# Gated attention and feed-forward on one core: V as 16 high and 15 low parts in one 32-column weight tile, with steps of 64 keys of eight heads

## The chip, the cores and the metric

The kernel runs on one core of one Trainium2 chip. The metric is the time of one execution on the device in microseconds (us). Three runs of the kernel before gave a median of 1062.46 us (1061.37 to 1062.55).

## The reference

```python
def reference(A_x, A_wq, A_wk, A_wv, A_wo, B_x, B_w1, B_w2, gate_w):
    q = (x @ wq).reshape(B, S, H, Dh).transpose(0, 2, 1, 3)
    k = x @ wk
    v = x @ wv
    scores = einsum("bhqd,bkd->bhqk", q, k) * (Dh ** -0.5)
    p = softmax(scores, axis=-1)
    o = einsum("bhqk,bkd->bhqd", p, v)
    a = o.transpose(0, 2, 1, 3).reshape(B, S, H * Dh) @ wo
    h = silu(einsum("bsd,df->bsf", x, w1))
    b = einsum("bsf,fd->bsd", h, w2)
    g = sigmoid((x * gate_w).sum(-1, keepdims=True))
    return g * a + (1 - g) * b
```

x is 2048 x 512 (S = 2048 positions, D = 512), there are H = 32 heads of Dh = 16, one key and one value head for all of them, and F = 1792 features in the feed-forward part. Everything is f32. The result has to be as precise as f32 products, so the kernel writes most operands as a sum of a high and a low 16-bit part and multiplies three times (high x high, high x low, low x high).

## The kernel before

**Engines.** TensorE (PE) multiplies, ScalarE (ACT) takes exponentials, VectorE (DVE) splits, normalises and adds, SyncE (SP) issues most DMAs, GpSimd (POOL) clears tiles and issues the loads of weights. Each works through its own list in order. The order on every engine is written out by the kernel.

**Start.** `first_pass` loads x, transposes it, makes K and V for all positions, the first blocks of Q and bounds for the exponent's shift. `V(c)` (L419 to L425) transposes V into `VF`, an f32 tile of 16 key blocks by 32 columns: 16 columns of V and a column of ones, which gives the softmax's sum. `v_parts` (L342) makes `VH` and `VL`, its high and low f16 parts. Q goes to DRAM (`qd`) and comes back through `load_q` (L260), which fills a tile `qb` with high and low parts for both halves of the partitions; `sh` holds the shifts.

**Attention.** 512 queries (c) of eight heads (o) make a Q block. `rounds` (c, o, rb) has 32 entries: each is four of these eight heads, and its steps go over 16 key blocks of 128 keys, so that there are 512 steps. A round's heads are spread over the two row halves of the array (f) and two tiles in turn (p). In a step `scores` (L1018) multiplies K by Q twice (j = 0, 1; eight matmuls of 32 keys each, one of eight places of the array each, which run side by side), into the PSUM tile S (two buffers), and ACT takes exp of it into P (f32, 128 keys by four heads by 512 queries, four buffers). `pv` (L1058) multiplies P with V, one matmul for each of four heads and each half of the 128 keys, so the two halves of the keys stand in two PSUM tiles, `pv0` and `pv1`.

**Split and native steps.** The loop takes two steps in a turn (256 turns in all). The second step of a turn is always native: one f32 pass with `VF`. The first is split where DVE has room (`split_step`): the upper 16 bits of P, read as bf16 in place (`upper`, a stride of two), are multiplied by `VH` and by `VL`, and the low part L = P - upper(P), made by DVE in f16 (`low`, L1053), by `VH`. A step over the first key block of a round is native.

**Slots.** A turn's order on PE is a string: S is a score block, F an eight-matmul slot of the other work (feed-forward, Q blocks, output projection), P a pass of the split step before, B a bound, N a native pass. `SPLIT = "SFFFSFFFSPPPSBN"` is the plain one; `DENSE` and `WIDE` ones have more F. After each turn `fill` (L794) issues waiting DVE work against a budget in us: the evictions' second halves, weight splitting (`split_pieces`), checks of ranges (`chores`), and the rest of the normalising.

**A round's end.** `norm_a` (L970) transposes `pv0` and `pv1` into T and U, adds them, takes the reciprocal of the sum column and multiplies, into half of C. After the second of two rounds `norm_b` transposes C and `norm_c` splits it into O for the output projection. At a round's start `prefetch` issues the load of the next round's Q tile.

**Second pass.** If a range check fails, the whole is done again with scales taken from the data. It doesn't run with these inputs.

## Time and profile before

| | |
|---|---|
| median of three runs | 1062.46 us |
| span of the profiled execution | 1063.5 us |
| PE busy | 1047.1 us (98%) |
| ACT busy | 1013.2 us (95%) |
| DVE busy | 821.4 us (77%) |
| POOL busy | 26.8 us (3%) |
| exp (L1031) | 1024 instructions, 972.0 us busy |
| low parts (L1053) | 194 instructions, 443.2 us busy |
| PV passes with f16 or bf16 (L1075) | 3 x 1552 matmuls |
| granted TensorE clock, mean | 0.995 |

A line of the timeline has a start in us from the span's start, a length in us, the engine, the line of the kernel, the operation, what it writes and reads, the shapes, and how many like instructions were merged; in brackets stands an idle time of the engine ahead of it and what ended it. A group's line has the busy time in us and the mean length of one in ns, then the idle time ahead of its instructions. Matmuls of one slot run side by side in eight places of the array, so the length of one says little; the distance from one slot's start to the next is what a slot costs.

### The profile page before, as it was taken

To read this page: it belongs to the slowest core of one execution; us is meant where nothing else is said; L and a number is where in the kernel's file an instruction comes from. 1 tells how busy PE (TensorE), PEld (TensorE's weight loads), DVE (VectorE), ACT (ScalarE), POOL (GpSimd) and SP (SyncE) were. 2 spreads that over 40 slices of the span, in tenths; PEclk is the share of its full clock that TensorE was granted. 3 is DMA by queue.
4 is the path that set the end of the run, shared out by engine and by line. 5 is a ranking of instruction groups with operands and counts; after the bars stand their busy time and mean duration, and the time that the engine had idled before them with its cause. 6 is when DMAs were issued, how large, how long until landed. Compare 5 with 4: busy or idle time off the path is not lost.

```text
span 1063.5 us, 66447 instructions
## 1 busy us (share of the span) xinstructions
PE 1047.1 (98%) x31517; PEld 662.6 (62%) x31517; DVE 821.4 (77%) x925; ACT 1013.2 (95%) x1118; POOL 26.8 (3%) x56
## 2 busy tenths in 40 slices
PE   8999999999999999999999999999999999999996
PEld 6575777755555577665765567676665575555753
DVE  6787888878887788888888697887887774757775
ACT  6899999999999999999999999999999999999993
POOL 1110010000000000000000000000000000000000
PEclk9999999999999999999999999999999999999998
DMA  6322111100001000000000000000000100000001
GB/s 222 115 61 61 51 47 53 50 21 22 4 21 41 21 23 10 16 11 22 13 11 31 29 26 12 12 22 12 18 8 12 41 22 11 12 11 5 12 4 44
DMA packets 20706, 32.99 MB, mean 31 GB/s; under 512 B 5001, under 2 KB 11914, under 8 KB 20426
## 3 DMA queue, kind: packets, MB, share of 16 engines
q1 hardware_dynamic: 17338, 20.20, 5.8%
q0 software_dynamic: 2512, 8.13, 2.6%
q8 instruction: 248, 4.06, 1.6%
q10 hardware_dynamic: 576, 0.33, 0.1%
q14 instruction: 32, 0.26, 0.1%
HBM read 20.12 MB, written 8.52 MB: 27 GB/s over the span
## 4 chain that ended last, share of the span: by engine, by line
PE 92%; ACT 3%; DVE 2%; DMA 1%; issue 0%; SPq 0%; DVEq 0%; ACTq 0%
PE pv L1075 36%; PE pm L778 33%; PE S L1028 20%; ACT P L1031 3%; DMA xn<-in_A_x_dram 1%; PE pm L782 1%; PE pk L395 1%; PE pt L321 0%; DVE T L974 0%; DVE mxs L139 0%; DVE U L975 0%; DVE acc L759 0%; DVE T L976 0%; DVE C L981 0%; PE pm L352 0%
## 5 line engine op out<-in xcount | busy, mean ns | idle before, releaser
L1031 ACT ACTIVATE P<-S 128x1024 f32<-128x1024 f32 x1024 | 972.0, 1051 | 19.8 <-PE S L1028 7.7
L1028 PE MATMUL S<-qb,KT 50*32 50x512 f16 x8192 | 477.7, 378 | 1.1 <-ACT P L1031 1.0
L1053 DVE TENSOR_TENSOR L<-P 128x2048 f16<-128x2048 f32 x194 | 443.2, 2285 | 44.5 <-ACT P L1031 44.2
L1075 PE MATMUL pv<-P,VF 64*32 64x512 f32 x5088 | 353.4, 589 | 0.0
L1028 PEld LDWEIGHTS <-KT 50*32 50x32 f16 x8192 | 191.6, 90 | 188.7 <-issue 120.8
L778 PE MATMUL pm<-w2s,H 64*32 64x512 f16 x5376 | 268.4, 375 | 0.7 <-DVE e L827 0.4
L778 PE MATMUL pm<-xs,w1s 64*32 64x512 f16 x5376 | 244.2, 375 | 0.8 <-DVE acc L759 0.8
L778 PEld LDWEIGHTS <-H 64*32 64x32 f16 x5376 | 143.6, 93 | 47.5 <-issue 13.0
L778 PEld LDWEIGHTS <-w1s 64*32 64x32 f16 x5376 | 136.1, 93 | 43.5 <-issue 11.8
L1075 PEld LDWEIGHTS pv<-P,VF 64*32 64x32 f32 x5088 | 115.2, 107 | 29.7 <-issue 6.7
L827 DVE SCALAR_TENSOR_TENSOR e<-e,pm 128x512 f32<-128x512 f32 x56 | 38.5, 687 | 82.1 <-ACT e L826 81.8
L1075 PE MATMUL pv<-P,VH 64*32 64x512 bf16 x1552 | 91.7, 388 | 0.0
L1075 PE MATMUL pv<-P,VL 64*32 64x512 bf16 x1552 | 91.3, 385 | 0.0
L1075 PE MATMUL pv<-L,VH 64*32 64x512 f16 x1552 | 89.6, 374 | 0.2
L778 PE MATMUL pm<-xs,wqs 64*32 64x512 f16 x1152 | 81.4, 375 | 0.6 <-DVE qx L862 0.6
L1075 PEld LDWEIGHTS <-VH 64*32 64x32 f16 x3104 | 64.9, 93 | 22.5 <-issue 1.5
L778 PE MATMUL pm<-wo_s,O 64*32 64x512 f16 x1440 | 63.4, 375 | 0.0
L974 DVE STREAM_TRANSPOSE T<-pv 128x512 f32<-128x512 f32 x32 | 23.0, 717 | 41.4 <-PE pv L1075 30.1
L759 DVE SCALAR_TENSOR_TENSOR acc<-pm,g,acc 128x512 f32<-128x512 f32 x47 | 35.0, 744 | 19.6 <-PE pm L778 19.4
L778 PEld LDWEIGHTS <-wqs 64*32 64x32 f16 x1152 | 39.7, 92 | 13.1 <-issue 4.4
L125 DVE TENSOR_TENSOR H<-e,H 128x512 f16<-128x512 f32 x56 | 38.8, 692 | 1.9
L1075 PEld LDWEIGHTS <-VL 64*32 64x32 f16 x1552 | 32.6, 94 | 11.2
(162 smaller groups left out, 466.7 us busy)
## 6 DMA issues: line engine op xcount, KB each, us to landing
qb<-qd SPq DMA_DIRECT2D x192, 32.0 KB
raw<-in_B_w_dram POOLq DMA_DIRECT2D x23, 256.0 KB, 3.0
xn<-in_A_x_dram SPq DMA_DIRECT2D x8, 512.0 KB
out_dram<-acc SPq DMA_DIRECT2D x15, 256.0 KB
qd<-qx SPq DMA_DIRECT2D x12, 256.0 KB
raw<-in_A_wo_dram POOLq DMA_DIRECT2D x4, 256.0 KB, 3.2
qb<-sh SPq DMA_DIRECT2D x62, 2.0 KB
raw<-in_B_w_dram SPq DMA_DIRECT2D x3, 256.0 KB
```

Of the source, the lines that this page charges most:

```text
L125: nc.vector.tensor_tensor(a2, a, a1, op=OP.subtract)
L395: nc.tensor.matmul(pk[64 * h:64 * h + 64], wkvs[:, i, kt], xs[:, j, kt, (c + h) * 512:(c + h) * 512 + 512], start=kt + n == 0, stop=kt == ...
L759: nc.vector.scalar_tensor_tensor(a, po, gate[:, n:n + 1], a, op0=OP.mult, op1=OP.add)
L778: nc.tensor.matmul(self.bank[32 * m:32 * m + 32], l(i, rows, 32 * m), r(j, rows), start=first, stop=last)
L782: nc.tensor.matmul(self.bank, l(i, slice(0, 128), 0, 128), r(j, slice(0, 128)), start=first, stop=last)
L827: nc.vector.scalar_tensor_tensor(e, e, 1.0, ph, op0=OP.add, op1=OP.mult)
L974: nc.vector.transpose(T, pv[0])
L1028: nc.tensor.matmul(sc[32 * m:32 * m + 32, f], KT[b:b + 50, k0:k0 + 32], qtile[i][b:b + 50, j], start=True, stop=True)
L1031: nc.scalar.activation(P[:, 2 * j:2 * j + 2], sc, AF.Exp, scale=scale_of(c, o))
L1053: nc.vector.tensor_tensor(lows[s], P, upper(P), op=OP.subtract)
L1075: nc.tensor.matmul(pvs[i][h][32 * j:32 * j + 32], a[r], b[r, j], start=first, stop=last)
```

## The change

V's low part gets into the 32 columns that a weight tile has anyway: column 0 is ones, columns 1 to 16 the high parts of V's 16 columns, and 17 to 31 low parts of the first 15. The sixteenth low part is written into the others: `v_parts` rounds the high parts to a common grid for each key and moves small multiples of the grid's step from low columns to high ones, so that a sum of column 16 and the first twelve low columns with weights 1, -1/2, -1/4 ... (`nus`; formed by `norm_x` and `norm_y`) gives the sixteenth column back. So a split step needs two passes, upper(P) and the low part, both with the one tile `VP`.

With high and low columns of the same keys side by side, a step now takes 64 keys of all eight heads, not 128 keys of four: 16 rounds of 32 steps, 512 as before, and each half of the partitions holds the same keys for other heads. `VF` and `VP` have 32 key blocks, each stored in both halves; `V(c)` makes them by matmuls with the identity as the moving operand, 64 columns each. A Q tile holds eight heads (twelve DMAs, sixteen with shifts), and its prefetch is issued in the middle of a round. The low part of P goes into the lower 16 bits of P itself, as f16. V is packed inside the attention part (`pack`, with `fill`); a split step waits for it in the order (`packed`), so the first turns are native. Normalising is done once for eight heads, in three parts over several turns.

```diff
-SPLIT, NATIVE = "SFFFSFFFSPPPSBN", "SFFFSFFFSNBSN"
+SPLIT, NATIVE = "SFFFSFFFSPPSBN", "SFFFSFFFSNBSN"
...
-    VH = consts.tile([128, NKT, 32], F16)
-    VL = consts.tile([128, NKT, 32], F16)
-    VF = consts.tile([128, NKT, 32], F32)
+    NK = S // 64
+    VP = consts.tile([128, NK, 32], F16)
+    nus = consts.tile([128, 3, 16], F32)
+    VF = consts.tile([128, NK, 32], F32)
...
-    qb_ = [consts.tile([128, 2, 512], F16, name=f"qb{n}") for n in range(2)]
+    qb_ = [consts.tile([128, 2, 2, 512], F16, name=f"qb{n}") for n in range(2)]
...
+            for r in range(2):
+                nc.sync.dma_start(q[b:b + 16, r], v[f][:, r, :, 0])
+                nc.sync.dma_start(q[b + 16:b + 32, r], v[f][:, r, :, 0])
+                nc.sync.dma_start(q[b + 32:b + 48, r], v[f][:, r, :, 1])
+                if shifts:
+                    nc.sync.dma_start(q[b + 48:b + 48 + shifts, r], u[f][0:shifts, r])
...
+    def v_parts(tiles, half):
...
+        def first():
+            absmax(u, V)
+            nc.vector.tensor_scalar(u, u, 1.0 + 2.0 ** -9, 1e-30, op0=OP.mult, op1=OP.max)
+            nc.vector.tensor_scalar(u.bitcast(U32), u.bitcast(U32), 0x7F800000, None, op0=OP.bitwise_and)
+            ts(u, u, 2.0 ** -10)
+            ts(h, u, 0.5)
+            ts(m, u, MAGIC)
+            tt(hi, V, to(h), OP.subtract)
+            tt(hi, hi, to(m), OP.add)
+
+        def second():
+            tt(hi, hi, to(m), OP.subtract)
+            tt(lo, V, hi, OP.subtract)
+            tt(s, lo, nu, OP.mult)
+            nc.vector.tensor_reduce(w, s, axis=AX.X, op=OP.add)
...
+        def fifth():
+            tt(VP[:, these, 1:17], hi, k, OP.add)
+            tt(VP[:, these, 17:32], lo[:, :, 0:15], k[:, :, 0:15], OP.subtract)
...
-                pt = ps.tile([128, KD, 128], F32, name="pt", bufs=4)
-                for t in range(4):
-                    o = c * 256 + t * 128
-                    nc.tensor.transpose(pt[:, t], vr[:, o:o + 128], ident)
+                for a in range(2):
+                    pt = ps.tile([128, KD, 128], F32, name="pt", bufs=4)
+                    for t in range(4):
+                        o = c * 256 + a * 256 + t * 64
+                        for e in range(2):
+                            nc.tensor.matmul(pt[64 * e:64 * e + 64, t], vr[:, o:o + 64], ident, start=True, stop=True)
...
+            if extra:
+                extra.pop(0)()
+                room -= 1.8
...
-                    k0 = kt * 128 + 32 * m
-                    nc.tensor.matmul(sc[32 * m:32 * m + 32, f], KT[b:b + 50, k0:k0 + 32], qtile[i][b:b + 50, j], start=True, stop=True)
+                    k0 = kt * 64 + 32 * (m % 2)
+                    nc.tensor.matmul(sc[32 * m:32 * m + 32, f], KT[b:b + 50, k0:k0 + 32], qtile[i][b:b + 50, m // 2, j], start=True, stop=True)
...
-                lows[s] = wp.tile([128, 4, 512], F16, name="L", bufs=2)
+                lows[s] = half(probs[s], F16, 0)
...
-                nc.vector.tensor_tensor(lows[s], P, upper(P), op=OP.subtract)
+                nc.vector.tensor_tensor(lows[s], P, half(P, BF, 1), op=OP.subtract)
...
-                a = (VH, VL, VH)[n][:, k]
-                b = lows.pop(s) if n == 2 else upper(probs[s])
+                a = VP[:, k]
+                b = lows.pop(s) if n else half(probs[s], BF, 1)
...
+        def norm_a(pv, st):
+
+            st["T"] = wp.tile([128, 32, 32], F32, name="T2")
+            for n in range(2):
+                nc.vector.transpose(st["T"][:, 16 * n:16 * n + 16].rearrange("p a b -> p (a b)"), pv[n])
+
+        def norm_x(st):
+            T3 = st["T"]
+            nc.vector.tensor_tensor(T3[:, :, 1:16], T3[:, :, 1:16], T3[:, :, 17:32], op=OP.add)
+            d = T3[:, :, 16:17 + DIG]
+            w = st["w"] = wp.tile([128, 512], F32, name="U")[:, 0:32 * (1 + DIG)].rearrange("p (a b) -> p a b", a=32)
+            nc.vector.tensor_tensor(w, d, nus[:, 1:2, 0:1 + DIG].to_broadcast([128, 32, 1 + DIG]), op=OP.mult)
+
+        def norm_y(st):
+            T3 = st["T"]
+            nc.vector.tensor_reduce(T3[:, :, 16:17], st["w"], axis=AX.X, op=OP.add)
+            r = wp.tile([128, 32, 1], F32, name="rr")
+            nc.vector.reciprocal(r, T3[:, :, 0:1])
...
+                norm_a(pvs.pop(i), state)
+                spend(1.4)
+                put(1.3, 1, lambda: norm_x(state))
+                put(1.6, 1, lambda: norm_y(state))
+                put(0.65, 3, lambda: (norm_b(state), put(1.0, 3, lambda: norm_c(state, (c, o)))))
...
+            if on and steps[s][1] == NKT:
+                prefetch(steps[s][0] + 1)
```

More of the change, by code (lines that the diff above doesn't have):

```diff
@@ L481, in first_pass @@
             next(q0)
[L482 removed]
+            load_q(qb_[0], 0, 0, 0)
             place(0)
@@ L604, in second_pass @@
             nc.vector.tensor_scalar(zsc, xk, -1.0, None, op0=OP.mult)
[L606 to L608 removed]
+            pv_ = ps.tile([128, NK, 32], F32, name="pv_", bufs=1)
+            for t in range(NK):
+                for e in range(2):
+                    nc.tensor.matmul(pv_[64 * e:64 * e + 64, t], kr[32:64, t * 64:t * 64 + 64], ident[32:64, 32:64], start=True, stop=True)
             vm = sb.tile([128, 1], F32)
@@ L1037, in split_step @@
         def split_step(s):
-            return steps[s][1] > 0 and backlog[0] < 0.8 and (dense_[0] or not (turn[0] and turn[0].hidden and (0 < turn[1] <= 6 or wide[0])))
+            return steps[s][1] < packed[0] and steps[s][1] > 0 and backlog[0] < 0.8 and (dense_[0] or not (turn[0] and turn[0].hidden and (0 < turn[1] <= 6 or wide[0])))
         def low(p, s, j):
@@ L1062, in pv @@
                 pvs[i] = [pO.tile([128, 512], F32, name=f"pv{h}") for h in range(2)]
-            first, last = k == 0 and n in (0, 3), k == NKT - 1
+            first, last = k == 0 and n in (0, 3), k == NK - 1
             if n == 3:
@@ L1093, in early_products, with pack @@
                 yield
+        def pack():
+            t2 = wp.tile([128, 32, 32], F32, name="T2").rearrange("p a b -> p (a b)")
+            tiles = [wp.tile([128, 512], F32, name="U"), t2[:, 0:512], t2[:, 512:1024]]
+            for half in range(2):
+                extra.extend(v_parts(tiles, half))
+                extra.append(lambda: packed.__setitem__(0, packed[0] + NKT))
+        packed, extra = [0], []
         qtile, wide = {}, [False]
```

143 lines of the change are left out of this document (78 added, 65 removed).

## The prediction, made before the changed kernel had run

> **What bounds the kernel now.** I read the page first, then ACT's timeline, then PE's timeline in one steady stretch, then DVE's groups and the two ends of the run.
>
> ```profile
> span 1063.5 us, 66447 instructions
> ...
> PE 1047.1 (98%) x31517; PEld 662.6 (62%) x31517; DVE 821.4 (77%) x925; ACT 1013.2 (95%) x1118; POOL 26.8 (3%) x56
> ...
> PE 92%; ACT 3%; DVE 2%; DMA 1%; issue 0%; SPq 0%; DVEq 0%; ACTq 0%
> ...
> L1031 ACT ACTIVATE P<-S 128x1024 f32<-128x1024 f32 x1024 | 972.0, 1051 | 19.8 <-PE S L1028 7.7
> ```
>
> The chain of work that ended last runs over PE for 92% of the span, so PE sets the pace. But ACT is busy for 95%. The question is how much room PE's shortening finds before ACT is the limit, and the next view answers it.
>
> ```profile
> 32.73 1.94 ACT L1031 ACTIVATE P<-S 128x1024 f32<-128x1024 f32 x2 [0.72 <-PE S L1028]
> ...
> 300.24 7.46 ACT L1031 ACTIVATE P<-S 128x1024 f32<-128x1024 f32 x8
> 307.51 0.67 ACT L826 ACTIVATE e<-pm 128x512 f32<-128x512 f32 x1
> 307.99 25.27 ACT L1031 ACTIVATE P<-S 128x1024 f32<-128x1024 f32 x27
> ...
> 964.11 79.75 ACT L1031 ACTIVATE P<-S 128x1024 f32<-128x1024 f32 x86
> ```
>
> The attention part lasts from the first exp at 32.73 to 964.11 + 79.75 = 1043.86 us. It has 1024 exps, four in each turn of the step loop (a turn is two steps of the loop over key blocks). When PE lets it, ACT does eight exps in 307.51 - 300.24 = 7.27 us, so 0.909 each and 3.64 a turn; a tanh adds 307.99 - 307.51 = 0.48 (4.12 a turn). The last row shows 79.75 / 86 = 0.927, so 3.71 a turn: there something other than ACT's own speed sets the pace. PE's rows of the same stretch show what.
>
> ```profile
> 1008.14 0.60 PE L1075 MATMUL pv<-P,VH 64*32 64x512 bf16 x8
> 1008.37 0.60 PE L1075 MATMUL pv<-P,VL 64*32 64x512 bf16 x8
> 1008.60 0.59 PE L1075 MATMUL pv<-L,VH 64*32 64x512 f16 x8
> 1008.84 0.57 PE L1028 MATMUL S<-qb,KT 50*32 50x512 f16 x8
> 1009.05 1.21 PE L1075 MATMUL pv<-P,VF 64*32 64x512 f32 x16
> 1009.91 0.57 PE L1028 MATMUL S<-qb,KT 50*32 50x512 f16 x8
> 1010.13 1.00 PE L778 MATMUL pm<-wo_s,O 64*32 64x512 f16 x24
> 1010.78 0.57 PE L1028 MATMUL S<-qb,KT 50*32 50x512 f16 x8
> ...
> 1011.87 0.59 PE L1075 MATMUL pv<-P,VH 64*32 64x512 bf16 x8
> ```
>
> Start to start: a PV pass of eight small matmuls takes 0.23 us (1008.14 to 1008.37), a score block S 0.22, three F slots 0.65 (0.217 each), a native f32 PV 0.86 (1009.05 to 1009.91, four f16 passes' worth). A whole turn is 1011.87 - 1008.14 = 3.73, and 4 x 0.22 + 6 x 0.217 + 3 x 0.23 + 0.86 = 3.73: PE is packed without a gap. PE at 3.73 and ACT at 3.64 are only 0.09 apart, which is the core of this case.
>
> **The removed pass.** In the built programs' instruction order both kernels have 256 turns, 194 split and 318 native steps. Each split step loses its VL pass: 194 x 0.23 = 44.6 us of PE. That is what PE gives up, not what the span gains. I price the 255 turns between the first exp and the last turn's first by kind (split or native first step; F slots; tanh or not), with PE's slots and ACT's times above, taking the larger.
> Before: 114 split turns with six F at 3.73 = 425.2; 44 native with six, 26 at PE's 3.90 and 18 with a tanh at ACT's 4.12 = 175.6; 66 split with eight F at 4.16 = 274.6; 15 native with eight at 4.33 = 65.0; 16 with fewer F or none = 60.0. Sum 1000.4. The trace gives 1043.86 - 1.05 (the last exp itself, the mean of L1031) - 32.73 = 1010.1, for an end that is the last exp's start: about 10 us over the ledger are stalls.
> After: the 114 fall to ACT's 3.64 = 415.0 (PE alone would do 3.50); the 44 stay 175.6; of the eight-F split turns 39 without a tanh fall to PE's 3.93 = 153.3 and 27 with one to ACT's 4.12 = 111.2; the 15 stay 65.0 and the 16 odd ones 60.0. Sum 980.1, 20.3 less.
> Two corrections. PE now runs ahead of ACT in split turns and can spend that lead (at most about half an exp, S having two buffers) in native or eight-F turns that follow: at most 26 x 0.26 and 27 x 0.19, together 12; I take 8, and keep 0 and 12. The 10 us of stalls I keep. A stall is mostly DVE being late with an eviction or a low part:
>
> ```profile
> 300.97 0.65 DVE L827 SCALAR_TENSOR_TENSOR e<-e,pm 128x512 f32<-128x512 f32 x1
> 301.54 2.27 DVE L1053 TENSOR_TENSOR L<-P 128x2048 f16<-128x2048 f32 x1
> ...
> 303.87 0.41 PE L1075 MATMUL pv<-L,VH 64*32 64x512 f16 x8
> ...
> 363.84 0.37 PE L778 MATMUL pm<-xs,wqs 64*32 64x512 f16 x1 [0.63 <-DVE qx L862]
> ```
>
> Here the low part ends at 303.81 and its pass starts at 303.87. With one pass less ahead of it PE asks for it 0.23 earlier, and turns are shorter; the instructions behind that wait are the next S, so ACT waits too. Against this, five chained normalising operations sit in DVE's queue ahead of such late low parts, 32 times now, and the change spreads them over three turns, 16 times. I put +2 on it, bounds -3 and +10. Attention: -20.3 - 8 + 2 = -26.3.
>
> **DVE's new work.**
>
> ```profile
> L1053 DVE TENSOR_TENSOR L<-P 128x2048 f16<-128x2048 f32 x194 | 443.2, 2285 | 44.5 <-ACT P L1031 44.2
> ...
> L974 DVE STREAM_TRANSPOSE T<-pv 128x512 f32<-128x512 f32 x32 | 23.0, 717 | 41.4 <-PE pv L1075 30.1 <-PE S L1028 11.3
> L975 DVE STREAM_TRANSPOSE U<-pv 128x512 f32<-128x512 f32 x32 | 21.6, 674 | 0.0
> ...
> L976 DVE TENSOR_TENSOR T<-T,U 128x272 f32<-128x272 f32 x32 | 14.2, 444 | 1.1
> L981 DVE TENSOR_TENSOR C<-T,rr 128x256 f32<-128x256 f32 x32 | 13.6, 425 | 1.1
> ...
> L978 DVE RECIPROCAL rr<-T 128x16 f32<-128x16 f32 x32 | 8.1, 254 | 1.1
> ...
> L139 DVE TENSOR_REDUCE mxs<-VF 128x1 f32<-128x256 f32 x1 | 0.4, 411 | 0.0
> ```
>
> The normalising costs 0.717 + 0.674 + 0.444 + 0.254 + 0.425 = 2.51 per round, 32 rounds = 80. After: two transposes, then 480, 416, 416 (a reduce), 32 and 512 elements; at the ~1.1 ns per element between these rows about 0.67 + 0.60 + 0.58 + 0.27 + 0.70, so 4.2 for 16 rounds = 67. Packing V costs, per half, about 13 operations of 256 elements (0.43), two reduces like L139 and ten tiny ones, priced as L978 (0.25): 8.9, twice 18 us. Net +4 on 821, in time that is idle. Until it is packed all steps are native: in turns 3 to 13 the built order has eleven native eight-F turns where six of these were split. They are in the counts above, and the split steps not done leave DVE six low parts (14 us) for the packing. One weight piece's second half now stands behind the first packing part (about 2 us): +1, bounds 0 and 2.
> The low part is written into P's own low halves, two bytes in four; no row shows such a write. The nearest is L1053, which reads P's upper halves with that stride at 2285 ns for 2048 elements: I take it as unchanged. From the other side no gain (one element per ns already), and a loss bounded by nothing in the trace; twice the time is the far end and a rival below. PE reading that stride is shown: pass to pass 0.23 from P, and no more.
> Mid-round prefetch of Q: sixteen SP issues instead of eight, but with half a round (eight turns, some 30 us) of cover, the same number in all. Nothing.
>
> **The start.**
>
> ```profile
> 21.80 0.66 PE L424 MATMUL pt<-ident,vr 128*128 128x128 f32 x4 [0.40 <-DVE xs L121]
> 22.39 2.78 PE L395 MATMUL pk<-xs,wkvs 128*64 128x512 f16 x24
> ...
> 30.00 2.32 PE L782 MATMUL pm<-xs,wqs 128*128 128x512 f16 x10
> 32.25 0.41 PE L1028 MATMUL S<-qb,KT 50*32 50x512 f16 x8
> ```
>
> ```profile
> 25.02 0.32 SPq L266 DMA_DIRECT2D qb<-qd  x1
> ...
> 27.25 0.42 SPq L268 DMA_DIRECT2D qb<-qd  x1
> 29.04 1.21 SPq L454 DMA_DIRECT2D qb<-s  x2
> ```
>
> PE: four f32 transposes of V (0.59 to the next row) become sixteen f32 matmuls with 64 columns. L395 shows 64-column matmuls of 512 at 2.78 / 24 = 0.116 (two at a time); f32 costs four times f16 (above), over a quarter of the elements: 16 x 0.116 = 1.9, so +1.25 for each of two V calls ahead of the first S: +2.5. One at a time it would be +2.9 each. SP: six loads from 25.02 to 27.67 (0.44 each) become twelve, to 30.3, then four shift loads at 0.605 to 32.7, against 30.25 before: also +2.5. The two run beside each other, and every later exp moves with the first: +2.5, bounds 1.9 and 5.8. POOL clears the Q tiles and V's tiles until
>
> ```profile
> 10.39 0.13 POOL L220 MEMSET VF<- 128x16 f32 x1
> ```
>
> and gets some 40 tiny memsets (0.13 each at most by that row) and twice the bytes: about 7 us more, done before the loads at 25.02.
> By the Trainium skill, "TensorEngine Tiling (Array Packing)", Gotcha 2, column tiling excludes the f32 transpose mode, which "TensorE: Matmul & The Clock Gate", Terms, puts at four times faster; by that the V calls would cost +8 and the sum some 6 us more. No run here shows it yet, and the rows' price is kept.
>
> **The end.**
>
> ```profile
> 1046.41 0.72 DVE L974 STREAM_TRANSPOSE T<-pv 128x512 f32<-128x512 f32 x1 [0.81 <-PE pv L1075]
> ...
> 1050.19 1.73 DVE L125 TENSOR_TENSOR O<-T,O 128x512 f16<-128x512 f32 x1
> ...
> 1050.21 0.89 PE L782 MATMUL pm<-wo_s,O 128*128 128x512 f16 x2 [0.92 <-DVE O L124]
> ```
>
> The last normalising is on the path: PE waits for O. It becomes 4.2 instead of 2.5 long, +1.7; two passes less at the end, -0.5: +1.2.
>
> **Sum.** -26.3 + 1 + 2.5 + 1.2 = -21.6 on the span of 1063.5: 1041.9. The profiled span lies 1.0 over the median of the runs (1062.46), so 1041.
>
> **Rivals.** (1) PE stays the bound, and ACT keeps up: all 44.6 come out, less 4.7 at the ends and in the early turns: 1022.6. For it: PE is packed without a gap. Against: 1024 exps at 0.909 and 56 tanhs at 0.48 are 958 us, and ACT can't catch up what it loses in tanh turns. (2) DVE's lateness becomes the pace: its share grows from 77% to 826 / 1042 = 79%, its queue is in order, and if half of the 194 low parts come 0.1 us late and the lead goes into that, +10 and +8 stand on the forecast: 1059. For it: the 0.06 us of spare at 303.81. Against: the bursts of normalising that made that wait are spread and halved. (3) Slower: the strided write makes L1053 dearer by x. DVE then needs 826 + 194x. If it can be kept busy for 90% of the span (an estimate; 77% now), it decides from 0.9 x 1042, x = 0.58, and the run is slower than before from 0.9 x 1063, x = 0.68; at twice the time it is (826 + 443) / 0.9 = 1410. For it: no row shows the write. Against: the strided read of L1053 leaves it at one element per 1.1 ns, like the dense rows. (4) The change doesn't pay at all, since PE's busy share says little: only 4.7 of new work shows, 1067.
> The Trainium skill ("Trainium Kernel Development and Optimization", Performance Expectations) says just that: matmul busy time is a bad metric, weight loads' busy share a good one, and that is 62% here. By it rival 4 holds. The start-to-start sum of 3.73 speaks against it, as does ACT's 0.927 where it can do 0.909.
>
> **Chances.** Forecast 0.67, rival 1 0.10, rival 2 0.13, rival 3 0.06, rival 4 0.04. Range: low end between the forecast with full lead and no extra stall (1041 - 4 - 5) and rival 1, 1028; high end with a start of +5.8 and DVE's +10 (1041 + 3 + 8) and most of rival 2: 1058. The measurement tells about 0.2% (2 us) from no change. Faster: forecast, rival 1 and most of rival 2, 0.87; same 0.03; slower: rivals 3, 4 and the rest of 2, 0.10.
>
> **What would show it.** Right: exps at 0.91 in split six-F turns with PE's rows waiting for "ACT P"; no VL pass left and 3104 matmuls on packed V; first exp near 35; the last transposes to the first L782 of the end 1.7 longer; L1053's successor at 2285. Wrong: exps still at 0.927 with a packed PE (rival 1 or stalls), PE rows released by the low part (rival 2), a low part over 2.5 us (rival 3), no change in the turn (rival 4).

## The result: 1.2% slower, and the profile after

The kernel after takes 1075.66 us (median of four runs, 1074.98 to 1076.03), the kernel before beside it 1062.51: a ratio of 1.0124, with a 95% interval of 1.011 to 1.0138. The forecast was 1041.0 in a range of 1028 to 1058, so the sign was wrong. The two profiled spans are 9.7 apart (1063.5 and 1073.2), less than the medians' 13.15. An execution's time is 1.8 longer than its span (1074.98 against 1073.2 for the profiled one of the kernel after), so the profiled execution of the kernel before took some 2.8 more than its median and the one after 0.7 less than its own. The 61 executions of the kernel before beside the experiments have spans of 1059.3 to 1062.2.

From the page of the kernel after: the span, the engines, the chain of waits by engine and by line, and groups (busy us, mean ns of one, then idle time ahead).

```profile
span 1073.2 us, 63489 instructions
...
PE 1039.6 (97%) x30021; PEld 570.7 (53%) x30021; DVE 888.3 (83%) x935; ACT 1012.1 (94%) x1118; POOL 30.2 (3%) x94
...
PE 65%; DVE 23%; ACT 7%; issue 3%; DMA 1%; SPq 1%; ACTq 0%; DVEq 0%
PE pv L1150 23%; PE pm L841 22%; PE S L1103 16%; DVE P L1128 13%; ACT P L1106 6%; DVE acc L822 1%; DVE T L1040 1%; ACT e L892 1%; PE pm L845 1%; DVE H L127 1%; DMA xn<-in_A_x_dram 1%; DVE e L893 1%; DVE qx L928 1%; DVE qx L927 1%; PE pk L450 1%
...
L1106 ACT ACTIVATE P<-S 128x1024 f32<-128x1024 f32 x1024 | 971.4, 1066 | 27.5 <-PE S L1103 14.7
...
L1128 DVE TENSOR_TENSOR P<-P 128x2048 f16<-128x2048 f32 x194 | 514.7, 2660 | 29.4 <-ACT P L1106 29.3
```

DVE has 23% of the chain, where it had 2%. The low parts (L1128) hold 13 of these 23%: 194 as before, but 2660 ns each in place of 2285. ACT's wait for S grew from 7.7 to 14.7 us.

The two ends of the attention part, from ACT's timeline:

```profile
35.10 1.94 ACT L1106 ACTIVATE P<-S 128x1024 f32<-128x1024 f32 x2 [1.17 <-PE S L1103]
...
972.78 79.45 ACT L1106 ACTIVATE P<-S 128x1024 f32<-128x1024 f32 x86
```

The first exp starts at 35.10 (32.73 before). The last group runs at 79.45 / 86 = 0.924 an exp, about as before (0.927). From the first exp's start to the last one's it is 1016.0 us, against 1010.0.

One place shows how the time is lost. DVE, PE and ACT after a round's end in the kernel after, one view for each:

```profile
364.73 1.31 DVE L1040 STREAM_TRANSPOSE T<-pv 128x512 f32<-128x512 f32 x2 [0.88 <-PE pv L1150]
366.07 0.66 DVE L1044 TENSOR_TENSOR T<-T 128x480 f32<-128x480 f32 x1
366.65 0.58 DVE L1047 TENSOR_TENSOR U<-T,nus 128x416 f32<-128x416 f32 x1
367.27 0.59 DVE L1051 TENSOR_REDUCE T<-U 128x32 f32<-128x416 f32 x1
367.77 0.34 DVE L1053 RECIPROCAL rr<-T 128x32 f32<-128x32 f32 x1
368.15 0.69 DVE L1055 TENSOR_TENSOR U<-T,rr 128x512 f32<-128x512 f32 x1
368.76 0.68 DVE L927 TENSOR_SCALAR qx<-pm 128x512 f16<-128x512 f32 x1
369.48 0.69 DVE L928 SCALAR_TENSOR_TENSOR qx<-pm,qx 128x512 f16<-128x512 f32 x1
...
370.28 5.18 DVE L1128 TENSOR_TENSOR P<-P 128x2048 f16<-128x2048 f32 x2
```

```profile
370.22 0.37 PE L841 MATMUL pm<-xs,wqs 64*32 64x512 f16 x1 [1.49 <-DVE qx L928]
...
372.98 0.42 PE L1150 MATMUL pv<-P,VP 64*32 64x512 f16 x8 [0.59 <-DVE P L1128]
```

```profile
371.35 1.95 ACT L1106 ACTIVATE P<-S 128x1024 f32<-128x1024 f32 x2 [1.46 <-PE S L1103]
373.68 3.94 ACT L1106 ACTIVATE P<-S 128x1024 f32<-128x1024 f32 x4 [0.39 <-PE S L1103]
```

The seven normalising operations stand back to back for 4.1 us, not over three turns. The eviction qx comes behind them; PE needs the tile that qx is read from (pm) and waits 1.49. Behind that, two low parts of 2.6 follow each other, and PE waits 0.59 for the first. S stands in PE's list behind each wait, so ACT idles for 1.46 and 0.39.

The end of the run: the last transposes on DVE, and the first product of the output projection on PE.

```profile
1054.51 1.31 DVE L1040 STREAM_TRANSPOSE T<-pv 128x512 f32<-128x512 f32 x2 [0.68 <-PE pv L1150]
```

```profile
1060.10 1.03 PE L845 MATMUL pm<-wo_s,O 128*128 128x512 f16 x2 [2.70 <-DVE O L126]
```

That is 5.59, against 1050.21 - 1046.41 = 3.80 before.

### The profile page after: what moved, and what is told of

The parts are those of the page before. It is cut to its first block, busy times and chain, and to the rows that moved or that the text cites. A ratio compares the mean times of both kernels' runs of the same rounds, so it can differ in the third digit from the quotient of the medians.

```text
span 1073.2 us, 63489 instructions
## 1 busy us (share of the span) xinstructions
PE 1039.6 (97%) x30021; PEld 570.7 (53%) x30021; DVE 888.3 (83%) x935; ACT 1012.1 (94%) x1118; POOL 30.2 (3%) x94
## 4 chain that ended last, share of the span: by engine, by line
PE 65%; DVE 23%; ACT 7%; issue 3%; DMA 1%; SPq 1%; ACTq 0%; DVEq 0%
PE pv L1150 23%; PE pm L841 22%; PE S L1103 16%; DVE P L1128 13%; ACT P L1106 6%; DVE acc L822 1%; DVE T L1040 1%; ACT e L892 1%; PE pm L845 1%; DVE H L127 1%; DMA xn<-in_A_x_dram 1%; DVE e L893 1%; DVE qx L928 1%; DVE qx L927 1%; PE pk L450 1%
## 5 line engine op out<-in xcount | busy, mean ns | idle before, releaser
L1106 ACT ACTIVATE P<-S 128x1024 f32<-128x1024 f32 x1024 | 971.4, 1066 | 27.5 <-PE S L1103 14.7
L1128 DVE TENSOR_TENSOR P<-P 128x2048 f16<-128x2048 f32 x194 | 514.7, 2660 | 29.4 <-ACT P L1106 29.3
L1103 PE MATMUL S<-qb,KT 50*32 50x512 f16 x8192 | 448.2, 379 | 1.7 <-ACT P L1106 1.2
L1150 PE MATMUL pv<-P,VF 64*32 64x512 f32 x5088 | 342.3, 589 | 0.0
L841 PEld LDWEIGHTS <-H 64*32 64x32 f16 x5376 | 126.9, 92 | 61.1 <-issue 19.4
L1150 PE MATMUL pv<-P,VP 64*32 64x512 bf16 (+1 forms) x3104 | 140.9, 388 | 9.5 <-DVE P L1128 8.8
L841 PEld LDWEIGHTS <-w1s 64*32 64x32 f16 x5376 | 114.8, 93 | 57.3 <-issue 10.7
L1150 PEld LDWEIGHTS pv<-P,VF 64*32 64x32 f32 x5088 | 100.0, 106 | 33.7 <-issue 6.8
L1150 PEld LDWEIGHTS <-VP 64*32 64x32 f16 x3104 | 61.3, 93 | 52.4 <-issue 27.7
L841 PEld LDWEIGHTS <-O 64*32 64x32 f16 x1440 | 27.9, 93 | 13.9 <-issue 1.6
L892 ACT ACTIVATE e<-pm 128x512 f32<-128x512 f32 x56 | 34.7, 619 | 0.0
```

The costliest lines, as they stand in the source:

```text
L841: nc.tensor.matmul(self.bank[32 * m:32 * m + 32], l(i, rows, 32 * m), r(j, rows), start=first, stop=last)
L892: nc.scalar.activation(e, ph, AF.Tanh, scale=t_scale)
L1103: nc.tensor.matmul(sc[32 * m:32 * m + 32, f], KT[b:b + 50, k0:k0 + 32], qtile[i][b:b + 50, m // 2, j], start=True, stop=True)
L1106: nc.scalar.activation(P[:, 2 * j:2 * j + 2], sc, AF.Exp, scale=scale_of(c, o))
L1128: nc.vector.tensor_tensor(lows[s], P, half(P, BF, 1), op=OP.subtract)
L1150: nc.tensor.matmul(pvs[i][h][32 * j:32 * j + 32], a[r], b[r, j], start=first, stop=last)
```

## The experiments

In this table "exps" is the distance from the first exp's start to the last one's in the profiled execution. The kernel before stood at 1062.1 to 1062.7 beside every run.

| kernel | median us | low part ns | DVE busy us | exps us |
|---|---|---|---|---|
| before | 1062.5 | 2285 | 821.4 | 1010.0 |
| after | 1075.7 | 2660 | 888.3 | 1016.0 |
| before, low part in place | 1074.8 | 2662 | 885.7 | 1021.6 |
| before, strided low part apart (one execution) | 1081.2 | 2663 | 889.3 | 1028.4 |
| before, two passes | 1052.0 | 2285 | 820.8 | 999.2 |
| before, two passes, low part halved | 1049.1 | 1218 | 615.2 | 995.5 |
| before, one pass, no low part | 1047.1 | none | 396.5 | 994.2 |
| after, low part of three blocks | 1061.4 | 2030 | 773.1 | 1002.5 |
| after, low part of two blocks | 1060.0 | 1395 | 647.2 | 1001.0 |
| the same, normalising at once | 1059.3 | 1395 | 649.8 | 1000.6 |
| the same, normalising cut short | 1055.6 | 1395 | 632.0 | 996.5 |

### The strided write, in the kernel before

```diff
-                lows[s] = wp.tile([128, 4, 512], F16, name="L", bufs=2)
+                lows[s] = probs[s].bitcast(F16).rearrange("p h (n two) -> p h n two", two=2)[:, :, :, 0]
```

> The kernel before with its low part written into P's lower halves as in the change, and nothing else. Theory A: the low part takes about 2660 ns, DVE is 72 us busier, and the time rises by 10 to 30 us (1072 to 1092). Theory B: the time stays within 4 us of the kernel before, even if the low part is dearer.

It took 1074.84, a ratio of 1.0115 (1.0098 to 1.0132). The group in its profile:

```profile
L1053 DVE TENSOR_TENSOR P<-P 128x2048 f16<-128x2048 f32 x194 | 514.6, 2662 | 27.5 <-ACT P L1031 27.3
```

That is the price in the kernel after, and with this one line alone the kernel before is as slow as the kernel after. PE's rows over the exps show the way: 24 times a matmul of the low pass starts more than 0.33 us after the one ahead, 7.8 us in all beyond a slot's 0.22 (3 times and 0.7 us in the kernel before, 32 times and 14.8 us in the kernel after). So late low parts make most of the 11.6 us. The second run asks whether it is the stride or the writing into P: the same stride into a tile of its own (f32 size, one buffer).

```diff
-                lows[s] = wp.tile([128, 4, 512], F16, name="L", bufs=2)
+                lows[s] = wp.tile([128, 4, 512], F32, name="L", bufs=1).bitcast(F16).rearrange("p h (n two) -> p h n two", two=2)[:, :, :, 0]
```

> The kernel before with its low part written with the same stride of two, but into a tile of its own (one buffer). It tells what makes the low part dearer, not the time of the kernel: if it is the stride of the write, about 2660 ns; if it is reading and writing the same tile, about 2285 ns.

```profile
L1053 DVE TENSOR_TENSOR L<-P 128x2048 f16<-128x2048 f32 x194 | 516.5, 2663 | 49.1 <-PE pv L1075 37.3
```

Again 2663: the stride does it, wherever it writes. The time of this one execution, 1081.21, also holds 37.3 us in which DVE waited for the single buffer.

### The removed pass alone

In the kernel before, the passes with `VL` are left out, and with them that product.

```diff
-SPLIT, NATIVE = "SFFFSFFFSPPPSBN", "SFFFSFFFSNBSN"
+SPLIT, NATIVE = "SFFFSFFFSPPSBN", "SFFFSFFFSNBSN"
...
-            slots, order = SPLIT, [(s - 2, 0), (s - 2, 1), (s - 2, 2), (s - 1, 3)]
+            slots, order = SPLIT, [(s - 2, 0), (s - 2, 2), (s - 1, 3)]
```

> The kernel before without its pass P times VL (that product is left out; nothing else is changed): the removed pass alone. Theory A: PE gives up 44 us, ACT's floor lets 20 to 28 of it through: 1034 to 1043, with exps at 0.91 in split turns of six F. Theory C (PE is not what sets the pace, so removing a pass can't pay): 1055 to 1063.

1051.99, a ratio of 0.9898 (0.9881 to 0.9914): between the two theories. The removed pass does pay, but the exps' part lost only 10.8 us, where my ledger had 20.3 and 8 of lead.

### DVE out of the way, by degrees

In the kernel after the low part is cut to three and to two of the four blocks; the pass reads a block twice, and the rest of P's low part is left out.

```diff
-                nc.vector.tensor_tensor(lows[s], P, half(P, BF, 1), op=OP.subtract)
+                nc.vector.tensor_tensor(lows[s][:, 0:3], P[:, 0:3], half(P, BF, 1)[:, 0:3], op=OP.subtract)
...
-                    nc.tensor.matmul(pvs[i][h][32 * j:32 * j + 32], a[r], b[r, j], start=first, stop=last)
+                    nc.tensor.matmul(pvs[i][h][32 * j:32 * j + 32], a[r], b[r, min(j, 2) if n == 1 else j], start=first, stop=last)
```

The run with two blocks has `[:, 0:2]` and `j % 2` there; the third does the same to the dense low part of the kernel before with two passes.

> The kernel after, whose low part covers three of the four blocks (the P V pass reads the third block's low part twice; the fourth's is left out). Everything on PE and ACT and every buffer stays as in the kernel after; only DVE's instruction gets shorter: 2660 x 3/4 = about 2000 ns, which is 285 less than the dense one of the kernel before. Theory A (the dearer strided write makes DVE late, and the lateness is what the span shows): the attention part falls by more than the 12 us that the strided write alone cost in the kernel before, so 1058 to 1063. Theory B (the order is at fault: with one pass less ahead of it PE asks for the low part 0.23 us earlier, whatever it costs): at most 4 us come back, 1072 or more.

> The kernel after, whose low part covers two of the four blocks (the P V pass reads them twice; the other two blocks' low parts are left out), some 1340 ns. It takes DVE out of the way and leaves PE and ACT as they are. Theory A: a second step of about the same price for each ns, so 1045 to 1055; if ACT's own speed is what is left (my ledger of 980 with the lead), about 1041 plus nothing. Theory B: 1070 or more.

> The kernel before without the pass over V's low part (that product left out), and with a dense low part over two of the four blocks (the other two left out), some 1160 ns. With the whole low part this kernel took 1052.0. If DVE's lateness is what kept the removed pass from paying its ledger (20 us on attention, up to 28 with the lead): 1036 to 1043. If the ledger itself was wrong, and ACT or PE hold the pace there: 1048 to 1052.

The group with three blocks:

```profile
L1128 DVE TENSOR_TENSOR P<-P 128x1536 f16<-128x1536 f32 x194 | 393.7, 2030 | 67.9 <-ACT P L1106 67.2
```

The 630 ns between 2660 and 2030 are worth 14.2 us; the next 635 are worth 1.4. DVE's price works like a step somewhere between 2030 and 2660 ns: below it the low part is mostly in time, and little is left to gain. Theory A holds for the first step and failed for the second, and theory B fell. But 1060.0 is 19 us above my forecast with DVE at 61%: the ledger was wrong too. The kernel before with two passes says the same: with half a low part 1049.1, outside the 1036 to 1043 that the ledger asked for and inside the 1048 to 1052 for a wrong ledger.

### PE's lead over ACT

The kernel before with the high pass alone in a split step:

```diff
-SPLIT, NATIVE = "SFFFSFFFSPPPSBN", "SFFFSFFFSNBSN"
+SPLIT, NATIVE = "SFFFSFFFSPSBN", "SFFFSFFFSNBSN"
...
-                nc.vector.tensor_tensor(lows[s], P, upper(P), op=OP.subtract)
...
-            slots, order = SPLIT, [(s - 2, 0), (s - 2, 1), (s - 2, 2), (s - 1, 3)]
+            slots, order = SPLIT, [(s - 2, 0), (s - 1, 3)]
```

> The kernel before with the high pass alone in split steps: the products with V's low part and with P's low part are left out, and with the latter DVE's low part. PE loses another 194 x 0.23 = 45 us against the run with two passes and half a low part (1049.1). My ledger let PE run up to half an exp ahead of ACT and spend this in native turns. In that run's trace S to exp takes 0.5 us and exp to the next S 0.2, which leaves at most 0.2 of an exp's 0.909 as a lead, used up by one native pass (1.08 from S to S). Theory H (no lead): native turns with six F and no tanh stay at 3.86 to 3.90, split turns with six F at 3.66 to 3.69; only split turns with eight F fall (from 4.03 to 3.7-3.8): 1036 to 1042. Theory L (lead was lacking because PE was still too full): these native turns fall to 3.64 to 3.70: 1031 or less.

1047.05, outside both ranges, and only 2.1 us under the run with two passes and half a low part, for another 45 us of PE's slots. The mean length of a turn by kind, in us, worked out from the start of every fourth exp:

| turn | ledger after | after | after, two blocks | before, two passes, half low | one pass |
|---|---|---|---|---|---|
| split, six F, no tanh | 3.64 | 3.77 | 3.72 | 3.69 | 3.69 |
| native, six F, no tanh | 3.90 less lead | 3.91 | 3.90 | 3.89 | 3.89 |
| split, eight F, no tanh | 3.93 | 4.21 | 4.06 | 4.03 | 4.00 |
| split, eight F, tanh | 4.12 | 4.23 | 4.17 | 4.17 | 4.17 |

Native turns stay at PE's 3.90, so theory H holds there and L fell. H's guess that split turns with eight F would drop to 3.7 or 3.8 failed as well: they take 4.00, though PE needs 3.70. PE's rows for S in such turns of the run with one pass, and ACT's group over thirteen of these exps:

```profile
371.54 0.41 PE L1028 MATMUL S<-qb,KT 50*32 50x512 f16 x8
372.62 0.41 PE L1028 MATMUL S<-qb,KT 50*32 50x512 f16 x8
373.70 0.41 PE L1028 MATMUL S<-qb,KT 50*32 50x512 f16 x8
374.78 0.41 PE L1028 MATMUL S<-qb,KT 50*32 50x512 f16 x8
375.87 0.41 PE L1028 MATMUL S<-qb,KT 50*32 50x512 f16 x8
376.34 0.41 PE L1028 MATMUL S<-qb,KT 50*32 50x512 f16 x8
```

```profile
365.35 13.00 ACT L1031 ACTIVATE P<-S 128x1024 f32<-128x1024 f32 x13
378.54 17.12 ACT L1031 ACTIVATE P<-S 128x1024 f32<-128x1024 f32 x17 [0.19 <-PE S L1028]
```

Five S in a row stand 1.08 apart: S itself takes 0.22, and four F (4 x 0.217) or a native pass (0.86) lie between two of them. ACT needs 0.909 an exp but gets (378.54 - 365.35) / 13 = 1.015. The start of the kernel after shows the delay from S to exp: S at 34.62, the exp at 35.10.

```profile
34.62 0.41 PE L1103 MATMUL S<-qb,KT 50*32 50x512 f16 x8
```

With two buffers of S, exp n must have read its tile before S n+2 is written, while exp n+1 runs for 0.909. S needs 0.48 to become an exp, so a lead is at most 0.909 - 0.48 = 0.43. In the trace of this run no S starts less than 1.07 us after the start of the exp that last read its tile, 0.16 more than the 0.909, which leaves 0.27. A gap of 1.08 uses 0.17 of it. Two such gaps use it up; only gaps shorter than 0.909 refill it. Four in a row, as in these rows, then cost 4 x 0.17 - 0.27 = 0.41 us over ACT's own time. By this the pace comes from the distances between S slots, not from the sum of a turn. The removed pass shortened one gap, 0.91 before, which was hardly too long. This is argued from the rows, not shown: no run moves the S slots alone or gives S a third buffer, and how much of the distance from 3.64 to 4.00 it makes stays open.

The trace agrees here with the Trainium skill ("Trainium Kernel Development and Optimization", Performance Expectations), which calls matmul busy time a bad metric: with one pass PE is still busy for 95% of the span, while 120 of its S wait for ACT.

```profile
L1028 PE MATMUL S<-qb,KT 50*32 50x512 f16 x8192 | 440.3, 380 | 33.9 <-ACT P L1031 27.3
```

### The normalising

With short low parts, the kernel after is still 5.5 us longer over the exps than the kernel before with two passes. PE in the run with two blocks, after the same round as above:

```profile
365.80 0.37 PE L841 MATMUL pm<-xs,wqs 64*32 64x512 f16 x1 [1.49 <-DVE qx L928]
```

The wait is as long as in the kernel after, though the low parts are half as long. Two edits of that run follow: normalising issued at once, and two of its operations left out (the product with `nus` and the reduce, so the sixteenth column of a head lacks its low part).

```diff
-                spend(1.4)
-                put(1.3, 1, lambda: norm_x(state))
-                put(1.6, 1, lambda: norm_y(state))
+                norm_x(state)
+                norm_y(state)
+                spend(4.3)
```

```diff
-            d = T3[:, :, 16:17 + DIG]
-            w = st["w"] = wp.tile([128, 512], F32, name="U")[:, 0:32 * (1 + DIG)].rearrange("p (a b) -> p a b", a=32)
-            nc.vector.tensor_tensor(w, d, nus[:, 1:2, 0:1 + DIG].to_broadcast([128, 32, 1 + DIG]), op=OP.mult)
...
-            nc.vector.tensor_reduce(T3[:, :, 16:17], st["w"], axis=AX.X, op=OP.add)
```

> The kernel after with a low part over two of the four blocks (as in the run that took 1060.0; two blocks' low parts left out), and with the normalising issued in one go at the end of its round, as in the kernel before, not over three turns. In that run's trace four turns after a round's end lose 0.8, 0.8, 0.8 and 1.5 us, in PE rows released by an eviction (qx or acc) that stands in DVE's queue behind the last normalising operations. Theory C (the spread normalising, put ahead of evictions, is the rest of the 5.5 us by which that run's attention part is longer than that of the two-pass kernel before): 2 to 4 us come back, 1056 to 1058. Its rival D (normalising delays something wherever it stands, in the kernel before too): 1059 to 1062.

> The kernel after with the low part over two of four blocks (1060.0), whose normalising leaves out the product with the digit weights and the reduce over it (column 15 of each head then lacks its low part): 0.59 + 0.59 of 4.2 us, 16 times. If the longer burst of normalising is what delays the evictions behind it (four turns with 0.8 to 1.5 us of stall): 2 to 4 us less, 1056 to 1058. If not, 1059 to 1060.

At once: 1059.28, with the intervals of the two ratios (0.9962 to 0.9982 and 0.9964 to 0.9985) on top of each other, so theory C fell. Both traces show why: from the first transpose to the last product 4.1 us in 12 of 16 rounds of the kernel after (4.6 to 5.0 in the other four, with other operations in between), in all 16 of the other run. They were hardly spread at all. Cut short: 1055.56, 4.5 us less for 16 x 1.18 us of DVE. The wait above, at the same place:

```profile
362.97 0.37 PE L841 MATMUL pm<-xs,wqs 64*32 64x512 f16 x1 [0.37 <-DVE qx L928]
```

The wait is 1.1 us shorter, as the burst is (3.0 instead of 4.1 us). DVE's load is not the reason: the step from three blocks of low part to two took 126 us off DVE for 1.4. So the length of the burst is what delays the evictions behind it.

### The low pass asked for later

Nothing is left out; the passes stand at the end of the turn, behind the native pass.

```diff
+LATE = {"SFFFSFFFSPPSBN": "SFFFSFFFSNSBPP", "SFFFFSFFFFSPPSBN": "SFFFFSFFFFSNSBPP", "SFFFFSPPSNSFFFF": "SFFFFSNSPPSFFFF"}
...
+            if 2 <= s and slots in LATE and steps[s - 1][1] != NK - 1:
+                slots, order = LATE[slots], [(s - 1, 3), (s - 2, 0), (s - 2, 1)]
```

> The kernel after with nothing left out and every instruction as it was, but the two passes of the split step stand behind the native f32 pass of the next step, at the end of the turn, so that PE asks for the low part about 0.86 + 0.22 = 1.08 us later (the last pair of each round keeps its order). Theory A1 (the low part of 2660 ns misses one point of the turn by some tenths of a us, and that is what the span shows): most of the 15 us that separate this kernel from the one with the short low part come back, 1058 to 1064. Rival A2 (DVE at 83% is behind in long stretches, so that a later point is missed just as well): 1070 to 1076. Rival: the buffer of P, held 1 us longer, stops the next exp: over 1076.

> The same move in the kernel before, nothing left out: three passes at the end of the turn. Its attention part has 7 us of stalls over the ledger of its slots, and the run with a short low part and two passes gained 3.7 against the whole low part. If the stalls are late low parts: 1055 to 1059. If they are late evictions and PE's packed order: 1061 to 1064.

After: 1069.67, between the two theories. Split turns with six F fell to 3.72, as with a short low part; those with eight F stayed at 4.25. So about 5 of the 15 us were lateness at one point of the turn, and the rest remains with a point 1.08 later. Before: 1062.46, no change (ratio 0.9994 to 1.0012), inside the range for late evictions and PE's packed order.

### Undoing the strided write in the kernel after

The room that the kernel after saves in P had gone to other tiles, so a dense tile needed space: one buffer, and two raw tiles for the weights in place of three; then the same as two half tiles; then the two raw tiles alone, as the control that the first run had lacked.

```diff
-    raw_ = [consts.tile([128, 512], F32, name=f"raw{n}") for n in range(3)]
+    raw_ = [consts.tile([128, 512], F32, name=f"raw{n}") for n in range(2)]
...
-                lows[s] = half(probs[s], F16, 0)
+                lows[s] = wp.tile([128, 4, 512], F16, name="L", bufs=1)
```

> The changed kernel with its low parts in a tile of their own again, written densely (one buffer, for want of space; one raw tile for weights less). Theory A (the write into every other two bytes of P made each low part 2660 instead of 2285 ns, and DVE's lateness ate the gain): low parts back at 2285, DVE 72 us less busy, the time falls to 1040 to 1052. Theory B (the other new work of DVE, packing and normalising, or the rounds of eight heads make the loss): the time stays at 1068 or more, whatever the low part costs.

> The kernel after with the low part as two dense instructions of two blocks each, in a tile of its own with two buffers (half the size each), and two raw tiles for the weights instead of three, which makes the room. Against the run with one dense tile (1086.0) it takes away most of the 53.9 us of waiting for that buffer. Theory A: 2 x 1.17 us of DVE in place of 2.66, so up to 12 us under the kernel after, less what the two raw tiles cost the early weights: 1064 to 1076. If the buffer is still waited for, 1076 to 1086.

> The kernel after with two raw tiles for the weights instead of three, and nothing else changed. If the two raw tiles made most of the 10 us of the runs with a dense tile: 1083 or more, all of it in the first quarter of the exps. If the wait for the single buffer made it: 1076 to 1078.

The medians are 1086.04, 1084.97 and 1093.70. The first two looked as if a dense write didn't help; the control shows that two raw tiles cost 18 us by themselves, all in the first quarter of the exps (282.1 us against 264.3). Against it the dense write gains 8 to 9 us, and the second and third quarter show 7 (257.3 + 253.5 falls to 253.0 + 250.9 with one tile, 253.1 + 251.0 with two half tiles). In the first quarter the one tile takes 3.6 us more than the control (285.7), the half tiles 0.6 less. The profiled execution of the one tile is the slowest of its four. The last try borrows the raw tiles when the weights are done (the second tile, of two halves, is left out here):

```diff
-                lows[s] = half(probs[s], F16, 0)
+                lows[s] = half(probs[s], F16, 0)
+                if not (split_pieces.left() or chores):
+                    lows[s] = [Ls[:, 0:4], (0, 4)], None
...
```

> The kernel after with nothing left out; as soon as the weights are split and the raw tiles are free (after some 220 us or a little more), the low part is written densely again, in turn into two raw tiles (one instruction, 2285 ns) and into the third raw tile and a new half tile (two instructions, 2 x 1219 ns); before that, into P as in the kernel after. The mean falls to about 2360 ns in the last three quarters. Theory A (price): with 2030 ns these quarters were 10.5 us shorter, with 2660 not at all, so 4 to 7 of them come back: 1069 to 1072. Rival (what made 1086 with one dense tile was the dense tile itself): 1076 or more.

> The same, with the two passes of the split step at the end of the turn, as in the run that took 1069.7. If lateness at one point and price are two ways to the same stalls, the gains do not add: 1066 to 1069. If they add: 1062 to 1065.

1074.83 and 1070.03. Both missed. The range checks, which use the raw tiles too, end late: the first dense low part starts at 840.8 us, and only 43 of the 194 became dense (18 of them as two halves).

```profile
L1135 DVE TENSOR_TENSOR P<-P 128x2048 f16<-128x2048 f32 x151 | 400.2, 2658 | 15.2 <-ACT P L1108 14.9
L1135 DVE TENSOR_TENSOR raws<-P 128x2048 f16<-128x2048 f32 x25 | 57.1, 2286 | 6.0 <-ACT P L1108 6.0
```

The dense ones fall into the last quarter of the exps, which takes 241.4 us in this kernel and in the kernel after alike. So the price of a low part matters only where the queue is late. The undo that reached the second and third quarter (above) did pay, and the later pass gains as much with it as without (5.1 us of exps, 4.9 in the kernel after).

### GpSimd as a helper

GpSimd takes two of the four blocks of a low part, first in the kernel after, then in the kernel before.

```diff
-                nc.vector.tensor_tensor(lows[s], P, half(P, BF, 1), op=OP.subtract)
+                for e, r in ((nc.vector, slice(0, 2)), (nc.gpsimd, slice(2, 4))):
+                    e.tensor_tensor(lows[s][:, r], P[:, r], half(P, BF, 1)[:, r], op=OP.subtract)
```

> The kernel after with nothing left out; GpSimd computes two of the four blocks of each low part, DVE the other two. DVE's share falls from 2660 to some 1400 ns. GpSimd's nearest row (the residual added by it, 512 f32 elements, 1402 ns) gives 2.8 us for its two blocks, which start with no queue ahead of them, so that both halves should be ready before the pass. If GpSimd keeps to that and does not slow DVE: 1060, as with the low part cut to two blocks, 0.2% under the kernel before. If GpSimd takes over 4 us a piece or slows DVE by sharing its path to memory: 1070 or more, and the pass waits for GpSimd.

> The kernel before with nothing left out; GpSimd computes two of the four blocks of each dense low part, DVE the other two (1218 ns in place of 2285). It tells how much of the kernel before was DVE's lateness: its attention part has 10 us over the ledger of PE's and ACT's slots. If DVE made them, most come back: 1053 to 1057. If PE's packed order made them, 1060 to 1063. If GpSimd is too slow or slows DVE, over 1066.

1068.22 and 1065.22, neither as hoped. Groups of the first run:

```profile
L1129 POOL TENSOR_TENSOR P<-P 128x1024 f16<-128x1024 f32 x194 | 474.8, 2447 | 436.1 <-ACT P L1106 391.1
...
L1129 DVE TENSOR_TENSOR P<-P 128x1024 f16<-128x1024 f32 x194 | 328.7, 1703 | 42.1 <-ACT P L1106 42.1
...
L127 DVE TENSOR_TENSOR H<-e,H 128x512 f16<-128x512 f32 x56 | 60.8, 1086 | 1.9
```

GpSimd takes 2447 ns, under the 2.8 us forecast, but DVE's half takes 1703 ns, not 1395, and an unrelated subtraction (H) 1086, not 692. In the kernel before, which gained nothing, DVE's dense half takes 1725, not 1218, and there operations with one input grow too: the first half of H (a cast, 512 elements) takes 903 ns, not 420. Operations that read a PSUM tile keep their length in both runs (`e<-e,pm` 687 ns and `acc<-pm,g,acc` 748 ns, with GpSimd and without, in the kernel after). The Trainium skill ("SBUF — State Buffer", Who interferes with whom) says that a DVE instruction with two inputs in SBUF contends with a GpSimd instruction that reads SBUF; the trace agrees (1395 to 1703 ns).

## Why the prediction was wrong, step by step

**The low part, "I take it as unchanged": the step that failed.** It measures 2660, not 2285, and is worth +11.6 us of exps in the kernel before, more than the removed pass gained (10.8). The bound from the other side was named but given 0.06 as rival 3.

**Rival 3's threshold.** It let DVE decide from x = 0.58, on the estimate that DVE "can be kept busy for 90% of the span". The run was slower already at x = 0.375 with DVE at 83%. An average busy share says little of an in-order queue whose bursts (4.1 us of normalising, 1.4 of qx, 2 x 2.66 of low parts) are longer than a turn.

**The removed pass, -20.3, and the lead, -8.** The pass alone gave -10.8. Of the missing 17.5 us, 3.7 come with DVE's lateness (999.2 against 995.5), near the +2 put on it. The rest is the ledger: it took the larger of PE's and ACT's sum for a turn and let a lead carry over. This is the second step that failed: 28.3 forecast, 10.8 measured. Even with short low parts (1060.0) the time lies above the range of the forecast. The native turns show no lead, and eight-F turns stay at 4.00 with PE's sum at 3.70. That the distances of the S slots hold them there is argued, not shown.

**DVE's new work.** The price of one normalising was right (4.2 us). That it is spread over three turns was wrong; the longer burst costs 4.5 us by the run without two of its operations. Without the low parts DVE is 4.6 us less busy (378.2 before, 373.6 after), where the sum had +4. The early native turns and the packing: the first 256 exps take 259.4 us in that run and 257.6 in the kernel before with two passes and half a low part, 1.8 for a +1 with bounds 0 and 2. In the first 64 exps it is 3.2, and the next 192 give 1.4 back. No run isolates this term.

**The start, +2.5.** Measured +2.4. PE's and SP's rows of the kernel after, one view each:

```profile
21.49 1.97 PE L481 MATMUL pt<-ident,vr 128*64 128x128 f32 x32 [0.39 <-DVE xs L123]
23.29 2.76 PE L450 MATMUL pk<-xs,wkvs 128*64 128x512 f16 x24
```

```profile
30.26 2.23 SPq L516 DMA_DIRECT2D qb<-s  x4
```

The V call takes 1.80 from its start to the next row's (each f32 matmul has two records), for the forecast 1.9, and SP's loads end at 32.5 for 32.7. The estimate from the Trainium skill ("TensorEngine Tiling (Array Packing)", Gotcha 2, with "TensorE: Matmul & The Clock Gate", Terms) was 8 for the two calls; the trace doesn't agree: 1.80 - 0.59 = 1.2 each.

**The end, +1.2.** In the two profiles it is +1.4 from the last exp's start to the end (22.1 against 20.7), but that is luck in part. From the last transposes to the first product it grew by 1.8, for the forecast 1.7. The profile of the kernel before has a long end: the twelve matmuls of its last projection start over 4.1 us, with a granted clock of 0.79 from 1048 to 1056 us. In six runs with the same end they start over 2.4 us (clock 1.00 in the run with late passes), and from the last exp to the end it is 18.4 to 19.0. With the new end these matmuls take 3.7 to 4.7 in eleven of twelve kernels (clock 0.66 from 1056 to 1066 us in the kernel after); why is not shown. Against those six ends the end after is 3.1 to 3.7 longer, not 1.4, and this makes some 2 of the 3.45 us between the spans' 9.7 and the medians' 13.15.

**What the runs give together.** For the exps: -10.8 for the pass, +11.6 for the strided write, +4.5 for the burst, +1.8 for the early turns: +7.1, measured +5.9 (before rounding). With +2.4 and +1.4 that is the span's +9.7. The terms come from different kernels, so they need not add exactly, and the sum is that of two profiles, of which the one before was a long one. Rival 2's mechanism (late low parts and evictions) is what happened, with rival 3's dearer write behind most of it. The signs named for a wrong forecast stand in the trace: exps at 0.924, PE rows released by the low part, and a low part over 2.5 us. No version here that leaves nothing out is faster than the kernel before; what was not run is a dense tile with two buffers from the first turn on, beside three raw tiles.

## What to carry to other kernels

When an edit changes only where an elementwise result is stored, price the new access pattern by a run of that one edit before anything else; here it cost as much as a removed matmul pass gained (11.6 us of exps against 10.8). Where two engines hand tiles to each other through two buffers, compare the longest distances between the handing slots with the other engine's time for one tile, and not only the sums of a turn. And give an undo its own control where it needs room from somewhere else.

## What the hardware showed unexpectedly

- DVE writing f16 with a step of four bytes, from f32 input: 2660 ns for 2048 elements against 2285 dense. By the differences between sizes it is (2660 - 1395) / 1024 = 1.24 ns an element against (2285 - 1218) / 1024 = 1.04. One of its inputs was strided in both cases. A pass of PE that reads P with this stride takes 0.23 us to the next slot; a dense S or F slot takes 0.22.
- While GpSimd computes half of the low parts, DVE's operations between SBUF tiles can get much longer: in the kernel after 1395 to 1703 and 692 to 1086 ns with two inputs, in the kernel before 1218 to 1725 with two and 420 to 903 with one. Those that read PSUM keep their length (687 and 748 ns).
